# Two first weight loads moved from the SyncE queue to the ScalarE queue, in halves

## The chip, the cores and the metric

The kernel runs on one core of one Trainium2 chip. The core has TensorE (in the profile PE for its matmuls, PEld for its weight loads), VectorE (DVE), ScalarE (ACT), GpSimd (POOL) and SyncE (SP, which here does nothing but issue DMAs). Every engine takes its instructions strictly in order. The metric is the device time of one execution in microseconds (us).

## The reference

Three stages follow one another, all in float32. First windowed attention over 4 batches, 8 heads and 576 positions of 64 values, where a query sees itself and the 63 positions before it:

```
scores = where(mask, scale * q @ k.T, -1e9);  attn = softmax(scores);  x = attn @ v
```

Then, on the 2304 tokens of 512 values, a dense layer with a rational activation:

```
h = x @ w_in                                   # 512 -> 2048
P = a0 + a1*h + a2*h**2 + a3*h**3
Q = 1 + |b0|*|h| + |b1|*h**2
y = (P / (Q + 1e-6)) @ w_out                   # 2048 -> 512
```

Last a mixture of 8 experts, where each token goes to one expert: `out = gate * sigmoid(...) * (relu(y @ w1[e]) @ w2[e])`.

## The kernel before

Tokens are cut into 9 blocks of 256. Attention works in units: a block and a pair of heads, four units to a block, 36 in all. `at_T` transposes q and k of a unit on TensorE (tile `tq`) and copies them out (`kT`, `qbd`, both kept in the tile `KK`), `at_QK` forms the scores (`sc`), masks them on VectorE (`ms`, `mn`, line 343), takes their exponential on ScalarE (line 349) and scales them by the reciprocal of their sum (`sg`, lines 352 and 353, and a product on GpSimd, line 173), `at_PT` transposes them (`pp`), and `at_PV` multiplies by v (`xp`) and stores the block's x as a high and a low part (`x0` for the first block, `xh` and `xl` later).

The dense layer uses split weights: each product is made of three matmuls of high and low parts (`mm3`). So every piece of `w_in` and `w_out` is first loaded raw (tile `stg`, 1 MB, 128 partitions by 2048 words, function `load_w`) and then converted in two halves (`convert`): three VectorE steps on 128x512 words (lines 288, 290, 292; tiles `cp`, then `ct`), a rounding copy for the high part (line 167 or 169) and a difference for the low part (line 173), into `wi` or `wo`. The first half of a raw piece of `w_in` is its tile's first two slices, the second half the last two. There are 16 such pieces; `cseq` gives their order, the first four being pieces of `w_in`.

A step s of the dense layer is one block and one piece: `rt_mm1` (tile `h`), an activation on ScalarE, VectorE and GpSimd (`rt_head`, `rt_inv`, `rt_tail`, `rt_gsplit`, tiles `e`, `t`, `qm`, `r`, `g`), and four steps later `rt_mm2` (tile `y`).

The body at the end of the function emits all this in a written order, with priorities (`later`); a scheduler then lays the instructions of each engine out by a timeline of its own costs, so what stands in a queue is not the written order. Which engine does an operation is fixed while the code is emitted (`pick`). All loads of the first stage stand in SyncE's queue; eight completion semaphores serve the plain DMAs in turn, and a DMA waits until the one before it on its semaphore has landed.

Line 961 loads the first raw weight piece with `c_load(1)`; the second is loaded from `c_conv`, which calls `c_load(m + 1)` and `c_load(m + CA)`. Line 964 is ScalarE's first small operation, the absolute value of the two numbers b.

Of the kernel before, what the change touches and what calls it, by code (L numbers as in the profile page):

```python
# [12 lines left out]
AF = mybir.ActivationFunctionType  # L13
# [23 lines left out]
def kernel(  # L37
# [16 lines left out]
    nc = tc.nc  # L54
# [45 lines left out]
    cs, co, npre, CNT, CN2 = [cols[x] for x in ("cs", "co", "npre", "CNT", "CN2")]  # L100
# [19 lines left out]
    def t8(shape, name, dt=F32R):  # L120
        return w8.tile(shape, dt, tag="w8", name=name)
# [134 lines left out]
    pos = {jf: s for s, jf in reversed(list(enumerate(seq)))}  # L256
    ffirst = [pos[0, fp] for fp in range(NFP)]

    def load_w(n):
        kind, fp = cseq[n]  # L260
        if kind == 0:
            t = t8([128, KD, 512], "stg", U32)
            src = w_in_u[:, fp * 512:(fp + 1) * 512]
        else:
            t = t8([128, 2, 1024], "stg", U32)
            src = w_out_u[fp * 256:(fp + 1) * 256, :]
        nc.sync.dma_start(out=t, in_=src.rearrange("(k p) f -> p k f", p=128))
        for i in range(2):
            r = t[:, 2 * i:2 * i + 2, :] if kind == 0 else t[:, i, :]
            stg[kind, fp, i] = (r[:, :, 0::2], r[:, :, 1::2]) if kind == 0 else (r[:, 0::2], r[:, 1::2])  # L270
# [608 lines left out]
    cpos = [0, 0]  # L879

    def c_load(n):
        while cpos[0] < min(n, len(cseq)):
            load_w(cpos[0])
            cpos[0] += 1
# [25 lines left out]
    def qk_upto(m):  # L910
        while loaded[0] <= min(m, NUNIT // 2 - 1):
            load_qk(loaded[0])
            loaded[0] += 1
# [44 lines left out]
    nc.sync.dma_start(out=cs, in_=cst[:, :C_TRI])  # L958
    v_upto(0)
    qk_upto(1)  # L960
    c_load(1)
    for t in qbd:
        nc.gpsimd.memset(t, 0.0)
    nc.scalar.activation(out=co[:, 4:6], in_=co[:, 4:6], func=AF.Abs)

    def prepare():
        wgs = t2([128, KD, 2 * E], "wgs")
# [194 lines left out]
```

## Time and profile before

| | us |
|---|---|
| median of 3 runs | 808.91 (808.74 to 809.58) |
| the profiled execution | 810.46 |
| its span, first to last instruction | 808.5 |
| TensorE busy | 766.3 |
| VectorE busy | 539.0 |
| ScalarE busy | 506.3 |
| GpSimd busy | 449.9 |

The span is what the profile covers; 2.0 us of the profiled execution lie around it. A share of busy time is a mean over stages with different limits, so the tables by stretch below matter more than these sums. In the timeline, the number in square brackets is how long the engine sat idle before the instruction, and the name behind the arrow is what ended the idle time.

### The profile page before, as it was taken

What the parts mean: (1) busy time and instruction counts of PE and PEld (TensorE: products, weight loads), DVE (VectorE), ACT (ScalarE), POOL (GpSimd) and SP (SyncE); (2) the same over time, 40 slices, a digit from 0 to 9 for tenths busy, and PEclk for the clock granted to TensorE, in tenths of its full rate; (3) what the DMA queues carried; (4) which work ended last, traced back from release to release, by engine and by line L of the source; (5) the groups of instructions that cost most, each with busy time, mean ns of one, the idle gap of its engine ahead of it and who ended that gap; (6) DMA issues with size and microseconds to landing.
All of it is one profiled execution on the core that took longest, in us unless ns stands there. A gap on an engine that the chain in (4) does not pass through costs nothing. (4 is left out here: it accounts for less than half of the span.)

```text
span 808.5 us, 15245 instructions
## 1 busy us (share of the span) xinstructions
PE 766.3 (95%) x5456; PEld 690.8 (85%) x5456; DVE 539.0 (67%) x1289; ACT 506.3 (63%) x1122; POOL 449.9 (56%) x399
## 2 busy tenths in 40 slices
PE   5868999999999999999999999897998999999994
PEld 4758899888899899999999998786997999999993
DVE  5799999876776766666676667465655456654630
ACT  5889786997766686676676665673525555543420
POOL 2596786665555555565654654675523554556430
PEclk9999999999999999999999999998998999999997
DMA  9786351422321211112120000323618777767610
GB/s 227 223 234 180 92 183 79 131 77 57 84 67 27 51 54 37 41 53 53 27 67 14 1 27 1 101 84 97 243 50 328 273 234 213 239 228 257 212 55 14
DMA packets 105602, 95.26 MB, mean 118 GB/s; under 512 B 77424, under 2 KB 77808, under 8 KB 105520
## 3 DMA queue, kind: packets, MB, share of 16 engines
q1 hardware_dynamic: 101840, 84.49, 35.1%
q0 software_dynamic: 3680, 9.73, 3.2%
q8 instruction: 45, 0.74, 0.4%
q14 instruction: 37, 0.30, 0.1%
HBM read 83.02 MB, written 11.44 MB: 117 GB/s over the span
## 5 line engine op out<-in xcount | busy, mean ns | idle before, releaser
L178 PE MATMUL y<-wo,g 128*128 128x512 f32 x864 | 220.1, 402 | 4.3 <-POOL g L173 3.3
L178 PE MATMUL h<-xh,wi 128*128 128x256 f32 x1024 | 195.8, 284 | 0.0
L178 PEld LDWEIGHTS y<-wo,g 128*128 128x128 f32 x864 | 158.4, 191 | 35.8 <-POOL g L173 3.5
L178 PEld LDWEIGHTS h<-xh,wi 128*128 128x128 f32 x1024 | 164.4, 192 | 2.7 <-DVE xl L388 0.2
L178 PE MATMUL h<-xl,wi 128*128 128x256 f32 x512 | 145.9, 285 | 0.0
L173 POOL TENSOR_TENSOR wx<-wr,wx 128x1024 fp32r<-128x1024 f32 x31 | 83.6, 2707 | 59.8 <-ACT wx L167 51.2
L173 POOL TENSOR_TENSOR g<-t,g 128x512 fp32r<-128x512 f32 x72 | 93.0, 1294 | 40.1 <-ACT g L167 34.8
L178 PE MATMUL hp<-xdh,wx 128*128 128x256 f32 x576 | 109.9, 290 | 3.8 <-ACT xdh L786 3.7
L173 POOL TENSOR_TENSOR qm<-qm,e 128x512 f32<-128x512 f32 x72 | 93.4, 1297 | 35.7 <-ACT qm L420 32.2
L178 PE MATMUL yp<-wx,hT 128*128 128x512 f32 x432 | 101.9, 392 | 0.0
L178 PEld LDWEIGHTS h<-xl,wi 128*128 128x128 f32 x512 | 98.3, 192 | 2.5
L178 PEld LDWEIGHTS hp<-xdh,wx 128*128 128x128 f32 x576 | 93.9, 198 | 5.3 <-ACT xdh L786 4.2
L415 ACT ACTIVATE e<-h 128x512 f32<-128x512 f32 x72 | 43.0, 597 | 87.3 <-PE h L178 87.1
L178 PEld LDWEIGHTS yp<-wx,hT 128*128 128x128 f32 x432 | 80.0, 188 | 16.4 <-DVE hT L794 0.3
L173 DVE TENSOR_TENSOR wx<-wr,wx 128x1024 fp32r<-128x1024 f32 x45 | 69.1, 1545 | 26.0 <-ACT wx L167 25.7
L167 ACT CAST wx<-wr 128x1024 fp32r<-128x1024 f32 x68 | 69.2, 1046 | 27.1 <-DMA wr<-in_moe_w_dram 21.8
L178 PE MATMUL hp<-xdl,wx 128*128 128x256 f32 x288 | 83.1, 290 | 0.7 <-DVE xdl L787 0.7
L440 DVE SCALAR_TENSOR_TENSOR t<-t,KK,r 128x512 f32<-128x512 f32 x72 | 53.6, 744 | 41.0 <-ACT r L434 40.6
L422 POOL TENSOR_SCALAR qm<-e,KK 128x512 f32<-128x512 f32 x45 | 34.6, 768 | 49.4 <-ACT e L415 49.2
L426 DVE TENSOR_TENSOR t<-t,h 128x512 f32<-128x512 f32 x72 | 49.1, 681 | 17.1 <-ACT t L416 17.0
L173 POOL TENSOR_TENSOR ms<-ms,sg 128x512 f32<-128x512 f32 (+4 forms) x60 | 39.2, 669 | 37.0 <-DVE sg L353 19.7
L433 ACT ACTIVATE r<-qm,KK 128x512 f32<-128x512 f32 x72 | 49.5, 688 | 15.3 <-POOL qm L173 14.7
(169 smaller groups left out, 1399.3 us busy)
## 6 DMA issues: line engine op xcount, KB each, us to landing
wr<-in_moe_w_dram SPq DMA_DIRECT2D x80, 512.0 KB, 4.8
stg<-in_moe_w_in_dram SPq DMA_DIRECT2D x8, 1024.0 KB, 6.7
stg<-in_moe_w_out_dram SPq DMA_DIRECT2D x8, 1024.0 KB, 7.4
v<-in_v_dram SPq DMA_DIRECT2D x58, 128.0 KB, 2.8
q<-in_q_dram SPq DMA_DIRECT2D x32, 128.0 KB, 2.8
k<-in_k_dram SPq DMA_DIRECT2D x32, 128.0 KB, 2.9
y_dram<-ysb SPq DMA_DIRECT2D x12, 256.0 KB, 2.1
yp_dram<-yq SPq DMA_DIRECT2D x6, 256.0 KB, 2.6
```

What stands on the lines that cost most here:

```text
L167: nc.scalar.copy(out=o, in_=i)
L173: (nc.vector if e == "D" else nc.gpsimd).tensor_tensor(out=o, in0=a, in1=b, op=op)
L178: pe[0] = nc.tensor.matmul(o, lhsT, rhs, start=start, stop=stop).ins
L415: nc.scalar.activation(out=e, in_=h, func=AF.Abs)
L422: (nc.vector if ef == "D" else nc.gpsimd).tensor_scalar(out=qm, in0=e, scalar1=co[:, 5:6], scalar2=co[:, 4:5], op0=ALU.mult, op1=ALU.add)
L426: nc.vector.tensor_tensor(out=t1, in0=t1, in1=h, op=ALU.mult)
L433: nc.scalar.activation(out=r0, in_=qm_t[s], func=AF.Ln, bias=qc_col)
L440: nc.vector.scalar_tensor_tensor(out=t1, in0=t1, scalar=co[:, 0:1], in1=r0, op0=ALU.add, op1=ALU.mult)
```

## The change

The first two raw weight pieces are no longer loaded by SyncE, one DMA of 1 MB each, but by ScalarE, two DMAs of 512 KB each. They stand right behind ScalarE's first small operation, and nothing else of ScalarE may come between (`issue_after`). The first half of a piece is what the first `convert` step reads, the second half what the second reads. The other 14 pieces are loaded by SyncE as before.

```diff
-    def load_w(n):
+    def load_w(n, eng=None):
...
-        nc.sync.dma_start(out=t, in_=src.rearrange("(k p) f -> p k f", p=128))
+        src = src.rearrange("(k p) f -> p k f", p=128)
+        if eng is None:
+            nc.sync.dma_start(out=t, in_=src)
+        else:
+            h = t.shape[1] // 2
+            for i in range(2):
+                eng.dma_start(out=t[:, i * h:(i + 1) * h], in_=src[:, i * h:(i + 1) * h])
...
-    c_load(1)
     for t in qbd:
         nc.gpsimd.memset(t, 0.0)
-    nc.scalar.activation(out=co[:, 4:6], in_=co[:, 4:6], func=AF.Abs)
+
+    with tc.issue_after(nc.scalar.activation(out=co[:, 4:6], in_=co[:, 4:6], func=AF.Abs).ins):
+        for n in range(2):
+            load_w(n, nc.scalar)
+    cpos[0] = 2
```

The scheduler lays the whole first part out anew. Lines below `load_w` move down by 6 in the changed program (9 at the end of the function), so line 288 becomes 294, and 343 becomes 349. VectorE's queue from its first copy of v, before:

```order
L169 COPY v<-v 64x256
L157 COPY KK<-tq 128x256
L159 TENSOR_SCALAR KK<-tq 64x4x64
L169 COPY v<-v 64x2x256
L169 COPY v<-v 64x256
L159 TENSOR_SCALAR KK<-tq 64x4x64
L343 ISA ms,mn<-sc,KK 128x64
```

and now:

```order
L169 COPY v<-v 64x256
L157 COPY KK<-tq 128x256
L159 TENSOR_SCALAR KK<-tq 64x4x64
L294 TENSOR_SCALAR cp<-stg 128x512
L159 TENSOR_SCALAR KK<-tq 64x4x64
L169 COPY v<-v 64x2x256
L169 COPY v<-v 64x256
L296 SCALAR_TENSOR_TENSOR cp<-stg,cp 128x512
L294 TENSOR_SCALAR cp<-stg 128x512
L349 ISA ms,mn<-sc,KK 128x64
```

The conversion of the first piece now begins ahead of the first unit's masks and ahead of one of the two copies of q (`qbd`) that line 159 makes. ScalarE's queue at its start, with what each row waits for, before:

```order
L964 ACTIVATE KK<-KK 128x2 [waits DMASW0_49]
L161 COPY KK<-tq 128x256 [waits PE_49]
L167 COPY v<-v 64x256 [waits DMAHW5_49]
L163 ACTIVATE KK<-tq 64x4x64 [waits DVE_49,Pool_49]
L163 ACTIVATE KK<-tq 64x4x64 [waits DVE_49]
```

and now:

```order
L970 ACTIVATE KK<-KK 128x2 [waits DMASW0_49]
L273 DMA stg<-in_moe_w_in_dram 128x2x512
L273 DMA stg<-in_moe_w_in_dram 128x2x512 [waits DMAHW0_49]
L273 DMA stg<-in_moe_w_in_dram 128x2x512 [waits DMAHW2_49]
L273 DMA stg<-in_moe_w_in_dram 128x2x512 [waits DMAHW4_49]
L167 COPY v<-v 64x256 [waits DMAHW5_49]
L161 COPY KK<-tq 128x256 [waits PE_49]
L163 ACTIVATE KK<-tq 64x4x64 [waits DVE_49,Pool_49]
```

Four DMAs stand ahead of ScalarE's copies, and the copy of v stands ahead of the copy of k. SyncE's queue where the second, third and fourth piece were loaded, before:

```order
L226 DMA k<-in_k_dram 128x4x64 [waits DMAHW5_49]
L267 DMA stg<-in_moe_w_in_dram 128x4x512 [waits DMAHW6_49]
L267 DMA stg<-in_moe_w_in_dram 128x4x512 [waits DMAHW7_49]
L226 DMA q<-in_q_dram 128x4x64 [waits DMAHW4_49,DMAHW5_49,DMAHW0_49,PE_49]
L226 DMA k<-in_k_dram 128x4x64 [waits DMAHW2_49,DMAHW3_49,DMAHW1_49,PE_49]
L226 DMA k<-in_k_dram 128x4x64
L226 DMA q<-in_q_dram 128x4x64
L267 DMA stg<-in_moe_w_in_dram 128x4x512
L267 DMA stg<-in_moe_w_out_dram 128x2x1024
```

and now:

```order
L226 DMA q<-in_q_dram 128x4x64 [waits DMAHW0_49]
L269 DMA stg<-in_moe_w_in_dram 128x4x512 [waits DMAHW1_49]
L226 DMA q<-in_q_dram 128x4x64 [waits DMAHW2_49]
L226 DMA k<-in_k_dram 128x4x64 [waits DMAHW3_49]
L226 DMA k<-in_k_dram 128x4x64 [waits DMAHW4_49]
L226 DMA q<-in_q_dram 128x4x64 [waits DMAHW5_49]
L269 DMA stg<-in_moe_w_in_dram 128x4x512 [waits DMAHW6_49]
L269 DMA stg<-in_moe_w_out_dram 128x2x1024 [waits DMAHW7_49]
```

Here the third piece stands behind q and k of the third pair of units instead of two pieces standing there, and the loads of q and k of the fourth pair no longer wait for TensorE.

## Rows read from the trace of the kernel before

**Rows 1.** The page: span, and busy time of each engine (share, instructions).

```profile
span 808.5 us, 15245 instructions
PE 766.3 (95%) x5456; PEld 690.8 (85%) x5456; DVE 539.0 (67%) x1289; ACT 506.3 (63%) x1122; POOL 449.9 (56%) x399
```

**Rows 2.** Busy time by stretch: stretch, its length, engines (instructions), granted clock, DMA share, GB/s.

```profile
core 0: us, PE busy (x) PEld busy (x) DVE busy (x) ACT busy (x) POOL busy (x), PEclk, DMA share, GB/s
...
10.00:20.00 10.00, 8.18 (x42) 7.40 (x42) 7.97 (x38) 7.64 (x26) 2.68 (x6) 0.90 1.25 266
20.00:30.00 10.00, 8.30 (x90) 6.78 (x88) 5.55 (x21) 8.25 (x32) 5.13 (x8) 0.93 0.97 298
30.00:40.00 10.00, 9.23 (x82) 8.39 (x83) 10.00 (x34) 8.39 (x29) 4.59 (x4) 1.00 0.49 159
40.00:60.00 20.00, 14.12 (x130) 12.16 (x128) 19.24 (x58) 17.11 (x51) 18.13 (x21) 1.00 0.87 228
60.00:80.00 20.00, 17.32 (x159) 15.84 (x160) 18.14 (x58) 19.78 (x65) 13.43 (x19) 0.91 0.73 190
...
100.00:200.00 100.00, 99.03 (x702) 89.34 (x701) 85.40 (x180) 84.40 (x182) 65.30 (x59) 1.00 0.33 105
7.63:32.48 24.85, 19.25 (x153) 16.31 (x153) 18.09 (x69) 18.43 (x65) 8.83 (x17) 0.93 1.09 293
...
4.79:7.28 2.49, 1.80 (x8) 1.43 (x8) 0.17 (x1) 0.01 (x2) 0.18 (x1) 1.00 1.11 234
```

**Rows 3.** Timeline of VectorE, 7 to 33 us: start, duration, instruction, [idle before <-releaser].

```profile
7.63 0.28 DVE L169 COPY v<-v 64x256 f32<-64x256 f32 x1 [2.03 <-DMA v<-in_v_dram]
...
8.18 0.41 DVE L159 TENSOR_SCALAR KK<-tq 64x256 f32<-64x256 f32 x1
...
11.30 0.23 DVE L343 CUSTOM_DVE_ANT_0 ms<-sc,KK 128x64 f32<-128x64 f32 x1 [1.51 <-PE sc L178]
...
12.25 1.29 DVE L288 TENSOR_SCALAR cp<-stg 128x512 uint32<-128x512 uint32 x2
...
18.00 0.22 DVE L343 CUSTOM_DVE_ANT_0 ms<-sc,KK 128x64 f32<-128x64 f32 x1 [0.52 <-PE sc L178]
...
22.43 0.17 DVE L352 TENSOR_SCALAR sg<-sg 128x4 f32<-128x4 f32 x1 [2.37 <-ACT ms L349]
...
27.41 0.17 DVE L352 TENSOR_SCALAR sg<-sg 128x4 f32<-128x4 f32 x1 [2.04 <-ACT ms L349]
...
27.49 0.69 DVE L288 TENSOR_SCALAR cp<-stg 128x512 uint32<-128x512 uint32 x1
...
31.80 0.68 DVE L292 SCALAR_TENSOR_TENSOR ct<-stg,cp 128x512 uint32<-128x512 uint32 x1
```

**Rows 4.** SyncE's queue, 0 to 26 us: DMA issues.

```profile
3.35 1.06 SPq L237 DMA_DIRECT2D v<-in_v_dram  x2
...
5.76 1.20 SPq L267 DMA_DIRECT2D stg<-in_moe_w_in_dram  x1
...
15.98 1.13 SPq L267 DMA_DIRECT2D stg<-in_moe_w_in_dram  x2
```

**Rows 5.** Tile `stg`, 0 to 60 us: SyncE's issue (ns, min/median/max); then, 0 to 10 us, the first piece's landing.

```profile
L267 SPq DMA_DIRECT2D stg<-in_moe_w_in_dram x4: 507/543/1198, 5.8 to 25.0; - x4
...
DMA to landing us min/median/max: 6.4/6.4/6.4
```

**Rows 6.** Tile `q`, 0 to 10 us: from issue to landing.

```profile
DMA to landing us min/median/max: 2.4/3.8/5.8
```

**Rows 7.** Timeline of ScalarE: its first operation, its first copy, and one wait at 44 us.

```profile
4.59 0.20 ACT L964 ACTIVATE KK<-KK 128x2 f32<-128x2 f32 x1 [2.56 <-DMA KK<-in_moe_b_dram]
...
7.28 0.37 ACT L161 COPY KK<-tq 128x256 f32<-128x256 f32 x1 [2.48 <-PE tq L308]
...
44.54 0.37 ACT L387 CAST xh<-xp 128x256 fp32r<-128x256 f32 x1 [1.35 <-PE xp L178]
```

**Rows 8.** Timeline of TensorE: its last long wait of the first part.

```profile
61.45 1.24 PE L178 MATMUL xp<-ms,v 128*64 128x64 f32 x32 [3.77 <-DVE t L442]
```

## Prediction

> **What bounds the kernel now.** I read the page first: TensorE is busy 766.3 of 808.5 us [rows 1]. The table by stretch says where the other 42 us lie. From 100 us on TensorE is full (99.03 of 100), while VectorE and ScalarE are busy some 85% [rows 2]: nothing that this change touches can matter there, except by letting TensorE arrive earlier. Before that TensorE waits: it is idle 1.82, 1.70, 0.77, 5.88 and 2.68 us in the stretches from 10 to 80 us [rows 2]. For whom is seen in the same rows: VectorE has no idle time at all from 30 to 40 us (10.00 of 10) and 0.76 us from 40 to 60; ScalarE is full from 60 to 80 (19.78 of 20). TensorE's longest wait there, 3.77 us at 61.45, ends with a VectorE step of the activation [rows 8]. So up to about 60 us VectorE sets the pace.
>
> Now the stretch before, VectorE's own timeline [rows 3]. From its first copy at 7.63 to the end of the second piece's last conversion step at 31.80 + 0.68 = 32.48 us it is busy 18.09 of 24.85 us [rows 2]: 6.76 us idle. Four waits make 6.44 of it: 1.51, 0.52, 2.37 and 2.04, two for scores, two for exponentials. While it waits there is conversion work that it could do, but the second piece is issued only at 15.98 [rows 4], and its first step runs at 27.49, directly behind the last of the four waits. The first piece was issued at 5.76 and took 6.4 us to land [rows 4, 5], so at 12.16, and its first step runs at 12.25: it too came as early as the load let it.
>
> **What the change does to the order.** What each engine does is unchanged: both programs have the same instructions on VectorE, ScalarE and GpSimd, apart from ScalarE's four DMAs. Only their order differs, and only at the front: the last 4,881 of 6,075 instructions in TensorE's queue, and the last 918 of 1,386 in VectorE's, stand alike. TensorE has 702 matmuls in the 100 us from 100 on [rows 2], so the common part begins somewhere near 160 to 175 us. As TensorE is full there, the end of the kernel moves by what TensorE's arrival moves. So the sum is what VectorE gains before 60 us.
>
> **The sum.** The new order has both loads' steps spread through the front of VectorE's queue: by the fourth `ct` it holds eight steps of the first two pieces ahead of the second reciprocal, against four before. The work to that point is the same but for one step, one x difference and four small operations that come later now; these cancel if both programs are compared at equal work. So VectorE would be 6.76 us earlier if it never stopped, and each stop in the new order is taken off.
>
> First stop: the step on the first half, now the fourth instruction from 7.63, behind `qbd`'s copy, which ends at 8.18 + 0.41 = 8.59 [rows 3]. ScalarE's first operation ends at 4.59 + 0.20 [rows 7], so the half is issued at about 4.85. The shortest landing of a small load there is 2.4 us [rows 6], the whole piece took 6.4 [rows 5]; half of the 4.0 between them added to 2.4 makes 4.4, so it lands at 9.2: 0.6 us lost. Bounds: nothing, if it lands by 8.59; 2.7, if it takes the whole piece's 6.4.
>
> Second stop: the masks of the third unit. Its scores stand behind the first unit's product with v in TensorE's queue now, so VectorE reaches them early. Bounds: nothing and 2.37, the longest wait of the four; I take the middle, 1.2.
>
> Third: later in the front the differences of x wait for ScalarE's casts of the third and fourth unit. In the trace such a cast waited 1.35 us for TensorE at 44.54 [rows 7]; the bounds are zero and what is left of the lead. I take 1.35, the one row of the kind.
>
> Fourth: the transfers. The second piece's 1.05 MB go ahead of loads of q, k and v that stood before them; at the 266 GB/s of that stretch [rows 2] that is 3.9 us, the upper bound. The lower is nothing, or less: the third pair's q and k now stand ahead of the third piece, and the fourth pair's no longer wait for TensorE. I take 0.8, near the lower end, because 10 to 20 us is the stretch in which none of the engines is full.
>
> ScalarE's issuing costs 4 x 0.543 = 2.2 us [rows 5] (no DMA of ScalarE's is in the trace; the bounds are 4 x 0.507 = 2.0 and 4 x 1.198 = 4.8). It lies between 4.79 and 7.28, in which ScalarE is busy 0.01 of 2.49 us [rows 2]: nothing. At 4.8 the first copy of k would begin 2.3 us late.
>
> 6.76 - 0.6 - 1.2 - 1.35 - 0.8 = 2.8 us. TensorE's idle time from 40 to 80 us, 8.56 us, has room for it. So has ScalarE's: it was idle 1.75 + 1.61 + 2.89 = 6.25 us from 20 to 60 us. The profiled execution took 810.46, 1.96 around its span; 808.5 - 2.8 = 805.7 for the span and 807.7 for such an execution. The median of the runs lies 1.55 below the profiled one: 808.9 - 2.8 = 806.1 us.
>
> All of it by bounds: no stop but the second's middle gives 6.76 - 1.2 = 5.6, so 803.3; every stop at its upper end (2.7, 2.37, 1.35, 3.9, and 2.3 for ScalarE) gives 12.6, a loss of 5.9.
>
> The stretch from 10 to 20 us has a DMA share over 1 [rows 2], so the engines that move the data have no room there. On that, "DMA: Bandwidth & Descriptors" of the Trainium skill (section Issuing engines are not separate DMA queues) speaks against this change: DMAs of several issuing engines interleave on the same 16 DMA engines, and a second issuer saves only the issue time. By that rule the gain from issuing is a few issues of 0.54 us; the rest of a gain would have to come from the place in the order. The trace of before has one issuer of such loads and can't show it.
>
> **Rivals.** *The transfers give it back (25%).* Two pieces are in flight at 7 us instead of one, and everything behind them lands up to 3.9 us later. For it: the full DMA share. Against it: from 15.98 on two pieces in a row were in flight before as well, and VectorE's waits were for scores and exponentials, not for loads. The fourth term at its upper end instead of 0.8: 6.76 - 0.6 - 1.2 - 1.35 - 3.9 = -0.3 lost, so 809 us, no change.
>
> *VectorE stands in order behind late halves: slower (15%).* Steps on the four halves now stand ahead of the masks of the first two units, which nothing held before. If the loads of SyncE and ScalarE took equal turns, 133 GB/s would be left for the halves: 0.52 MB then takes 3.9 us, and with 2.4 us ahead of them they land at 11.2, 15.1, 19.1 and 23. The second half's first step stands ahead of the first unit's masks, which ran at 11.30 [rows 3]: these would be 3.8 us late, and the second piece's steps would hold VectorE again. The fourth half's first step has some 8 us of VectorE's work ahead of it, so by 23 it would have been idle 23 - 7.63 - 8 = 7.4 us for the halves alone, and with the second and third terms 10 against 6.76: some 3 us slower, 812. It decides from the second half landing at about 14.4: 2.8 us past 11.6, where VectorE comes to it (9.2 and 2.4 us of steps). Against it: rows of weights are 2 KB in one piece and those of q, k and v 256 bytes, and 293 GB/s moved from 7.63 to 32.48 [rows 2]. The page named above (section Queues, rings and completion order) says that each DMA engine takes turns between the queues with work, packet by packet; by turns of equal size that is this rival, by turns of whole rows the weights come first.
>
> *ScalarE takes VectorE's place (part of the first case).* It is full from 60 us, so a lead of VectorE beyond what ScalarE can follow is lost. Its room of 6.25 us says that 2.8 passes; if its casts fall behind by the 2.2 us of issuing after all, 0.6 is left, 808.3.
>
> **How the numbers follow.** The forecast has 60%: 806.1, from 803.3 to 807.5. The first rival with its part 25%, 807 to 810; the slower one 15%, 809.5 to 813. About 0.2%, 1.6 us, is what a measurement of this kernel can tell from no change. Faster than 807.3: nearly all of the forecast's case and a little of the first rival's, 0.61. Within 1.6 us: 0.26. Slower than 810.5: most of the last case, 0.13. The range leaves out the best end and most of the slower case: 803.6 to 810.0.
>
> **What would show it.** Right: VectorE's steps on the first two pieces done by about 27 us instead of 32.5; its idle time from 7.63 to there nearer 2 than 6.76; TensorE's idle time from 40 to 80 us near 5.8 instead of 8.56; and the same distance from about 170 us to the end. First term: the first conversion step at 9.2, not past 10. Fourth: transposes of the third pair's q and k without a wait for a DMA. Wrong: the first unit's masks past 14 us with VectorE waiting for `stg`; or VectorE early and ScalarE full from 40 us on with TensorE as idle as before; or, against the whole argument, a different time in the part of the queues that stands alike.

## The result and the profile after

The changed kernel is 1.35% slower: 820.20 us median of 4 runs (818.56 to 820.83) against 809.25 of 4 runs of the kernel before (808.74 to 810.56), ratio 1.0135, 95% interval 1.0117 to 1.0152. Forecast were 806.1 us and a range of 803.6 to 810.0. The profiled execution took 820.49 us, with a span of 818.7.

Busy time by stretch of the changed kernel, columns as in [rows 2]:

```profile
7.63:32.48 24.85, 17.54 (x120) 14.81 (x121) 18.66 (x76) 17.25 (x61) 8.22 (x16) 1.00 1.04 287
10.00:20.00 10.00, 6.10 (x26) 5.41 (x27) 8.87 (x34) 5.43 (x22) 2.10 (x6) 1.00 1.09 286
40.00:60.00 20.00, 15.67 (x156) 14.12 (x158) 17.57 (x56) 17.84 (x53) 15.97 (x17) 0.93 0.83 212
60.00:80.00 20.00, 13.89 (x140) 12.31 (x136) 20.00 (x61) 17.09 (x53) 14.69 (x21) 0.93 0.58 154
80.00:100.00 20.00, 18.38 (x99) 15.15 (x98) 10.36 (x27) 9.19 (x28) 8.97 (x12) 0.81 0.40 98
100.00:200.00 100.00, 99.38 (x725) 90.28 (x724) 88.25 (x176) 85.16 (x181) 67.15 (x59) 1.00 0.36 112
```

The same stretch from 80 us in the kernel before, which was not shown above:

```profile
80.00:100.00 20.00, 20.00 (x150) 17.48 (x149) 19.38 (x41) 14.13 (x35) 15.80 (x19) 1.00 0.36 94
```

TensorE is idle 4.33 + 6.11 = 10.44 us from 40 to 80 us, where 8.56 were to shrink to 5.8, and 1.62 more behind 80, where it had no idle time. From 100 us on it is as full as before. The loss is therefore complete before the common part of the queues begins, and one small ScalarE operation of the router shows it well: the first `og`, which both programs reach inside the part in which TensorE is full. Here in the kernel before, then in the changed one (start, duration):

```profile
213.56 0.20 ACT L572 ACTIVATE og<-og 128x2 f32<-128x2 f32 x1
```

```profile
222.81 0.20 ACT L578 ACTIVATE og<-og 128x2 f32<-128x2 f32 x1
```

9.25 us later; the span is 10.2 longer. (The way from the first `og` to the end is not the same length in every execution, though the queues stand alike there: it took 594.9 us before and 595.9 in the changed kernel, and 591.7 to 595.9 over the thirteen executions in the table below whose row there is the same, all but n1 and n5. So the span of one execution decides nothing below some 4 us.) What lies in front of it is TensorE's timeline. The kernel before, 73 to 90 us (rows of `h` left out):

```profile
73.10 0.98 PE L178 MATMUL xp<-ms,v 128*64 128x64 f32 x16 [0.78 <-ACT ms L161]
74.52 0.63 PE L363 MATMUL pp<-KK,ms 128*128 128x128 f32 x4 [0.44 <-DVE mn L343]
74.90 3.02 PE L178 MATMUL y<-wo,g 128*128 128x512 f32 x12
...
80.63 1.09 PE L178 MATMUL y<-wo,g 128*128 128x512 f32 x4
81.66 0.98 PE L178 MATMUL xp<-ms,v 128*64 128x64 f32 x16
...
83.92 4.35 PE L178 MATMUL y<-wo,g 128*128 128x512 f32 x18
```

The changed kernel, 76 to 95 us:

```profile
76.08 0.98 PE L178 MATMUL xp<-ms,v 128*64 128x64 f32 x16 [1.05 <-ACT ms L161]
79.29 0.69 PE L314 MATMUL tq<-KK,k 128*128 128x128 f32 x2 [2.23 <-DVE mn L349]
...
80.31 1.09 PE L369 MATMUL pp<-KK,ms 128*128 128x128 f32 x4
83.03 1.52 PE L178 MATMUL xp<-ms,v 128*64 128x64 f32 x16 [1.62 <-ACT ms L161]
84.47 9.98 PE L178 MATMUL y<-wo,g 128*128 128x512 f32 x36
```

Before, the y matmuls are filler: runs of 12, 4 and 18 stand between the attention steps, and TensorE does not wait at all from 74.9 to 100. In the new order three more attention steps come first, TensorE waits 1.05, 2.23 and 1.62 us among them, and the first 36 y's follow in one run. And the clock falls, in the changed kernel and then in the one before over the same stretch:

```profile
77.50:87.80 10.30, 6.89 (x32) 5.15 (x33) 8.68 (x22) 7.75 (x24) 6.66 (x8) 0.50 0.46 130
```

```profile
77.50:87.80 10.30, 10.30 (x75) 8.93 (x74) 9.82 (x26) 9.30 (x27) 8.97 (x12) 1.00 0.38 103
```

A granted clock of 0.50 is the 1.2 GHz level; it came after the wait of 1.05 us and during that of 2.23. 16 matmuls of `xp` take 1.52 us there instead of 0.98.

### The profile page after: what moved, and what is told of

The parts are those of the page before. It is cut to its first block, busy times and chain, and to the rows that moved or that the text cites. A ratio compares the mean times of both kernels' runs of the same rounds, so it can differ in the third digit from the quotient of the medians.

```text
span 818.7 us, 15224 instructions
## 1 busy us (share of the span) xinstructions
PE 769.3 (94%) x5456; PEld 692.1 (85%) x5456; DVE 542.0 (66%) x1289; ACT 505.9 (62%) x1122; POOL 449.6 (55%) x399
## 5 line engine op out<-in xcount | busy, mean ns | idle before, releaser
L178 PEld LDWEIGHTS y<-wo,g 128*128 128x128 f32 x864 | 160.6, 193 | 35.8 <-POOL g L173 3.6
L173 DVE TENSOR_TENSOR wx<-wr,wx 128x1024 fp32r<-128x1024 f32 x45 | 73.1, 1634 | 25.6 <-ACT wx L167 25.3
L167 ACT CAST wx<-wr 128x1024 fp32r<-128x1024 f32 x68 | 69.3, 1047 | 27.4 <-DMA wr<-in_moe_w_dram 22.2
L355 ACT ACTIVATE ms<-ms,mn 128x128 f32<-128x128 f32 (+1 forms) x144 | 55.7, 391 | 5.7 <-DVE mn L349 2.8
```

The lines of the kernel that those rows point to most:

```text
L167: nc.scalar.copy(out=o, in_=i)
L173: (nc.vector if e == "D" else nc.gpsimd).tensor_tensor(out=o, in0=a, in1=b, op=op)
L178: pe[0] = nc.tensor.matmul(o, lhsT, rhs, start=start, stop=stop).ins
L355: nc.scalar.activation(out=ms[:, i, :nk[i]], in_=ms[:, i, :nk[i]], func=AF.Exp, scale=-1.0, bias=mn[:, i:i + 1], accum_out=sg[:, i:i + 1])
```

## The experiments

In most of them the order of the instructions on every engine (the "row") is held by hand, so that it can be kept while something else is changed. Each instruction is made to follow its neighbour in a list at the end of the file; the rest is the changed kernel:

```diff
+            line = [have[i] for i in order]
+            for a, b in zip(line, line[1:]):
+                tc.add_manual_dep(b, a.name, info, reason="hold")
```

| kernel | row | first loads | ratio to before (95%) | first `og`, us |
|---|---|---|---|---|
| before | its own | SyncE | 1 | 213.6 |
| changed | its own | ScalarE, halves | 1.0135 (1.0117 to 1.0152) | 222.8 |
| e1 | before | ScalarE, halves | 1.0001 (0.9978 to 1.0024) | 215.0 |
| e4 | changed | SyncE, whole | 1.0116 (1.0065 to 1.0167) | 224.9 |
| e2 | changed, v copies later | ScalarE, halves | 1.0102 (1.0053 to 1.0151) | 223.0 |
| h46 | changed to 46 us, then before | ScalarE, halves | 1.0015 (0.9991 to 1.0040) | 214.6 |
| h54 | to 54 us | ScalarE, halves | 0.9979 (0.9938 to 1.0019) | 213.6 |
| h66 | to 66 us | ScalarE, halves | 1.0048 (1.0022 to 1.0075) | 218.2 |
| h74 | to 74 us | ScalarE, halves | 1.0027 (0.9999 to 1.0054) | 218.3 |
| e5 | changed, 12 y's earlier | ScalarE, halves | 1.0065 (1.0043 to 1.0087) | 219.2 |
| e6 | e5, `sc` earlier | ScalarE, halves | 1.0075 (1.0047 to 1.0103) | 216.8 |
| e7 | e6, masks earlier | ScalarE, halves | 1.0038 (1.0012 to 1.0065) | 215.7 |
| n1 | planner's own | ScalarE, whole | 1.0121 (1.0092 to 1.0150) | 220.9 |
| n5 | planner's own | SyncE, whole | 1.0115 (1.0079 to 1.0151) | 222.2 |
| e8 | before, unpacking earlier | ScalarE, halves | 1.0034 (1.0014 to 1.0054) | 214.6 |

The last column is of one profiled execution each; the ratio decides. The times given below for "before" are its median in the same measurement.

**e1: the row of before, the loads of the change.** The list holds the order of before for all five engines; ScalarE's four DMAs stay.

> Nothing is left out. Every engine's instructions are held in the row in which the kernel before has them; only the first two weight loads differ, which ScalarE issues in halves behind its Abs, as in the changed kernel. Theory ORDER (what costs the 11 us is the new row of instructions that the planner makes after the edit, above all between 50 and 95 us): 806 to 811 us, near the kernel before, though the first copy of v still ends late. Theory CROWDING (what costs is that the halves on the second queue delay the first rows of v, k and q, and all engines start 2.5 us late): 815 to 820 us, near the changed kernel, with the first copy of v at about 10.1 us. Theory CLOCK (the stretches at the 1.2 GHz level between 77 and 88 us cost): goes with ORDER here, and those stretches are gone.

811.51 us against 810.84: no difference, with an interval of 1.9 us either way (the band for ORDER ended at 811). The edit by itself costs nothing and gains nothing that this interval can tell. The first copy of v was early, not late; but the loads do crowd another one, the k of the third unit, for which the transposes now wait (start, duration, [wait]):

```profile
14.52 0.44 PE L316 MATMUL tq<-KK,k 128*128 128x128 f32 x2 [1.82 <-DMA k<-in_k_dram]
```

**e4: the row of the change, the loads of before.** In the list of the changed kernel's order the two loads stand, whole, on SyncE behind its first eight DMAs:

```diff
-            load_w(n, nc.scalar)
+            load_w(n)
```

> Nothing is left out. Every engine's instructions are held in the row of the changed kernel, but the first two weight loads are whole again and issued by SyncE behind its first eight loads, so ScalarE issues none and v is not crowded. Theory CROWDING: 808 to 812 us, near the kernel before, with the first copy of v at about 7.6 us. Theory ORDER: 816 to 821 us, near the changed kernel, though the first copy of v is early, and TensorE idles and falls to its lower clock between 75 and 90 us again.

821.68 us, just above the band for ORDER: as slow as the changed kernel with nothing on ScalarE's queue. v is there at 7.43 us, and TensorE stands before the y's as it did:

```profile
85.10 1.52 PE L178 MATMUL xp<-ms,v 128*64 128x64 f32 x16 [3.31 <-ACT ms L161]
86.55 9.98 PE L178 MATMUL y<-wo,g 128*128 128x512 f32 x36
```

With e1 this settles the main question: the row costs some 10 us, the place of the loads nothing that these runs can tell.

**e2: v out of the way.** Only the first copies of v on VectorE and ScalarE are moved behind those of k and q.

```diff
 VectorE
-COPY v<-v 64x256
 COPY KK<-tq 128x256
 TENSOR_SCALAR KK<-tq 64x4x64
 ...
+COPY v<-v 64x256
```

> Nothing is left out. The changed kernel in its own row of instructions, but the first copies of v on VectorE and ScalarE stand behind the first copies of k and q, so that those do not wait for a late v. Theory CROWDING: VectorE's and ScalarE's first work begins 2 us earlier and most of the loss is won back, 809 to 814 us. Theory ORDER: the row behind 50 us is unchanged, 817 to 821 us, even where the first masks end earlier.

820.25 us. In the profiled execution of the changed kernel v had landed late, at 10.10 us instead of 7.63 [rows 3], and I had taken that for a cause. VectorE's first copy there:

```profile
10.10 0.28 DVE L169 COPY v<-v 64x256 f32<-64x256 f32 x1 [4.70 <-DMA v<-in_v_dram]
```

In the thirteen other profiled executions that copy v first it began between 7.08 and 7.71 us, and seven of them have the same loads in the same order. It was one execution's accident, and moving v wins nothing that shows.

**h54, h66, h74, h46: where in the row.** Each engine keeps the changed kernel's order up to what it had begun at 54 (66, 74, 46) us and takes what is left in the order of before.

```diff
-line = order of the changed kernel
+line = (its first n of each engine) + [the rest in the order of before]
```

> Nothing is left out. The changed kernel with ScalarE's loads in halves; each engine keeps the changed kernel's row up to what it has begun at 54 us, and from there takes what is left in the row of the kernel before. Theory ORDER, with the costly part behind 54 us: 805 to 811 us. Theory CROWDING, or ORDER with the costly part in front of 54 us: 816 to 821 us.

808.27 us against 810.84: the whole loss is gone, so it lies behind 54 us. In this kernel the first 12 y's start at 75.33 us, 0.4 behind before:

```profile
74.01 0.98 PE L178 MATMUL xp<-ms,v 128*64 128x64 f32 x16 [0.97 <-ACT ms L161]
75.33 2.99 PE L178 MATMUL y<-wo,g 128*128 128x512 f32 x12
```

Whether it beats the kernel before stays open: its interval takes in 1.

> Nothing is left out. ScalarE's loads in halves; each engine keeps the changed kernel's row up to what it has begun at 66 us there, and takes the rest in the row of the kernel before. Theory LATE (the loss arises behind 66 us, where TensorE waits in front of the 36 y's): 806 to 812 us. Theory MID (it arises between 54 and 66 us, where TensorE waits 2.84, 1.10 and 1.32 us): 814 to 820 us.

> Nothing is left out. As the kernel cut at 66 us, but cut at 74 us: only what begins behind 74 us stands in the row of before, the 12 y's in front of the waits at 77 us among it. Theory LATE: 807 to 813 us, and at least 5 us less than the changed kernel. Theory MID: 815 to 821 us, the loss being in the row by then.

> Nothing is left out. As the kernel cut at 54 us, but cut at 46 us: from there every engine has the row of the kernel before. Theory ORDER: 803 to 810 us, at most 0.2% above the kernel before. If the halves on ScalarE's queue do win time in front of 46 us, as was predicted, and the row of before keeps it, it is 0.2 to 0.6% below the kernel before; if the gain is lost behind 46 us in any row, it is within 0.2%.

813.87, 812.44 and 811.02 us against 809.70. The first lies between its two bands, 1.9 us above LATE and 0.1 below MID, so by itself it decides for neither. The second is in LATE's, and it stays some 1% below the changed kernel's ratio. So the row from 54 to 74 us carries some 0.3 to 0.5%, 2 to 4 us (the intervals allow 0 to 0.75%), and what begins behind 74 us most of the loss, some 7 to 9 of the 11. h46 is 1.0 us above its band in us and, at 0.15% over before, inside the one in per cent. It gains nothing over before: no gain of the loads that these runs can tell was hidden in front of 46 us.

**e5, e6, e7: the filler.** e5 moves 12 of the 36 y's on TensorE, in the row of the change; e6 also puts four `sc` in front of the other 24; e7 also puts four masks of VectorE in front of three unpacking steps.

```diff
 TensorE (e5)
 MATMUL xp<-ms,v 64x64 x8
+MATMUL y<-wo,g 128x512 x12
 MATMUL tq<-KK,k 128x128 x2
 ...
-MATMUL y<-wo,g 128x512 x36
+MATMUL y<-wo,g 128x512 x24
```

> Nothing is left out. The changed kernel, every instruction in its row, but for one move on TensorE: of the 36 matmuls into y that begin at 84.47 us there, the first 12 stand in front of the transposes that wait from 77.06 to 79.29 us. Theory FILLER (the loss arises where TensorE waits with y's ready behind the waiting instruction): the wait of 2.23 us goes, the clock does not fall there or for less long (at most some 3 us more), so 813 to 817 us. Theory WHOLE ROW (the loss is spread over the row of all engines behind 54 us, VectorE's above all, and the y's place is only its sign): 818 to 821 us, with the wait found again elsewhere before 90 us.

> Nothing is left out. As the kernel with the 12 y's moved, and the four sc matmuls that stand behind the h's at 97.16 us in the changed kernel are moved in front of the remaining 24 y's, so that VectorE, which idles 7.55 us for them, has its next masks about 10 us earlier. If VectorE's idle stretch there costs TensorE later (theory CHAIN): 2 to 5 us less than with the y's alone, 809 to 814 us. If TensorE is the bound from there on and VectorE's idle time is free: within 1 us of the kernel with the y's alone.

> Nothing is left out. As the kernel with the 12 y's and the four sc matmuls moved on TensorE, and on VectorE the four masks that stand between three conversions from 76.6 to 79.2 us stand in front of those three (1.9 us earlier). If VectorE's conversions among the masks carry the rest of the loss: TensorE's wait of 1.63 us for ms goes and the time falls by 1.5 to 4 us, 809 to 813 us. If not: 813 to 816 us, as without it.

e5: 815.88 us against 809.77. The ratio, 1.0065, is half of the changed kernel's 1.0135; against e2, the same row held with only v moved, 1.0102 shrank by a little over a third, and there the intervals overlap. So a third to a half of the loss goes with one move on one engine. The wait of 2.23 us is gone, though the granted clock is still 0.63 from 77.10 to 81.70, the lower level over most of the first 12 (4.61 us; 3.02 for as many before):

```profile
76.19 0.98 PE L178 MATMUL xp<-ms,v 128*64 128x64 f32 x16 [1.32 <-DVE t L435]
77.10 4.61 PE L178 MATMUL y<-wo,g 128*128 128x512 f32 x12
81.54 0.38 PE L316 MATMUL tq<-KK,k 128*128 128x128 f32 x2
...
84.20 0.98 PE L178 MATMUL xp<-ms,v 128*64 128x64 f32 x16 [1.63 <-ACT ms L161]
85.11 5.74 PE L178 MATMUL y<-wo,g 128*128 128x512 f32 x24
```

e6 (814.88 us against 809.77) is the same within the intervals, but it is no test of whether VectorE's idle time beside the y's costs anything. From 76 to 100 us VectorE was idle 24 - 16.51 = 7.49 us in e5 and 24 - 16.52 = 7.48 in e6: its longest wait there was 3.09 us for `sc` in e5 (up to 93.98 us), and it is 4.12 for ScalarE in e6 (up to 93.51).

e7 lies at 813.23 us against 809.70. The wait of 1.63 that it aimed at is still there, so its mechanism is refuted, and whether it is really 0.3% faster than e6 the intervals leave open:

```profile
80.71 0.98 PE L178 MATMUL xp<-ms,v 128*64 128x64 f32 x16 [1.63 <-ACT ms L161]
```

**n1, n5: the planner left free.** In n1 ScalarE issues each load in one piece; n5 issues at the same place in the program, but on SyncE.

```diff
 n1
-            h = t.shape[1] // 2
-            for i in range(2):
+            h = t.shape[1]
+            for i in range(1):
 n5
-            load_w(n, nc.scalar)
+            load_w(n)
```

> Nothing is left out. The changed kernel, but ScalarE issues each of the two loads whole and not in halves; the planner is left free and makes yet another row (the first y's in runs of 22, 18 and 8, with attention between them). Theory ORDER: the time goes by that row and not by who issues, anything from 804 to 816 us, and its excess over the kernel before equals TensorE's idle time up to 100 us over that before (20.06 us) plus what the half clock takes. Theory CROWDING (the second queue itself costs): 816 to 821 us.

> Nothing is left out. SyncE issues both loads whole, at the place in the program where the changed kernel has them, so no second queue; the planner is left free and makes its own row (first y's in two runs of 24, behind four attention steps). Theory ORDER: slower than before although no load is on ScalarE's queue, 811 to 821 us, with TensorE waiting in front of the first y's. Theory CROWDING: 807 to 811 us.

818.48 and 819.69 us against 809.77. Each small edit gets another row, with the first y's in runs of 22, 18 and 8 or of 24 and 24, and both rows are about 1% worse than that of before, with or without a second queue. n1 came out 2.5 us above the band that I gave for ORDER and inside CROWDING's; what speaks against CROWDING is e1, with ScalarE's loads and no loss, and n5, as slow with no load on ScalarE. The sum that I offered for n1 (idle time of TensorE to 100 us, and what the lower clock takes) can't be tested with these numbers: to 100 us n1 was busy 77.09 us against 79.94 before and reached `og` 7.3 us later, but h54 was busy 81.90 and reached `og` when before did, so busy time there does not count work (the part on the gain, below, shows why). Much of n5's loss is seen in its stretch from 60 to 80 us, in waits (6.77 us, where before had 2.68) and the lower clock:

```profile
60.00:80.00 20.00, 13.23 (x129) 11.75 (x128) 18.21 (x50) 15.47 (x48) 13.23 (x19) 0.74 0.33 90
```

**e8: VectorE's lead by force.** Open was why the forecast 2.8 us do not come in e1 either. e8 is e1 with the second load's four unpacking steps moved into VectorE's two long waits.

```diff
 VectorE
 SCALAR_TENSOR_TENSOR ct<-stg,cp 128x512
+TENSOR_SCALAR cp<-stg 128x512 x2
 TENSOR_SCALAR sg<-sg 128x4
 ...
+SCALAR_TENSOR_TENSOR cp<-stg,cp 128x512 x2
 TENSOR_SCALAR sg<-sg 128x4
-TENSOR_SCALAR cp<-stg 128x512 (x2), SCALAR_TENSOR_TENSOR cp<-stg,cp 128x512 x2
```

> Nothing is left out. The kernel in the row of before with ScalarE's loads in halves, and one move on VectorE: the four operations that unpack the second load (0.60 us each, 2.4 us, behind VectorE's second wait for ScalarE's ms at 27.41 us in the kernel before) stand in its two waits, two in front of the wait of 2.37 us that ends at 22.43 us and two in front of the one of 2.04 us that ends at 27.41 us. So VectorE is really 2.4 us ahead from 32 us on. Theory of the prediction (the end follows VectorE's lead): 2 to 3 us less than the kernel before, ratio 0.996 to 0.998. Theory ATTENTION (from 32 us on the end hangs on the attention steps and on x, which no earlier weight moves): within 0.2% of the kernel before, with the first activation of h less than 1 us earlier than in the same row without the move (47.1 us).

812.04 us against 809.25: not faster but 0.34% slower (0.14 to 0.54), so ATTENTION's band of 0.2% is missed as well, and whether it is slower than e1 the intervals leave open. The first activation of h runs at 47.1 us, as in e1. VectorE's waits, start, duration, [wait]:

```profile
24.52 0.17 DVE L360 TENSOR_SCALAR sg<-sg 128x4 f32<-128x4 f32 x1 [0.96 <-ACT ms L357]
...
29.54 0.17 DVE L360 TENSOR_SCALAR sg<-sg 128x4 f32<-128x4 f32 x1 [0.88 <-ACT ms L357]
...
31.73 0.42 DVE L396 TENSOR_TENSOR x<-xp,x 128x256 fp32r<-128x256 f32 x1 [1.38 <-ACT x L395]
```

The two waits (2.17 and 2.05 us in e1) shrink by as much as was put into them, 1.2 us each, and a third appears at once: VectorE runs up against the casts of x, which come out of attention. Of the lead of 2.4 us some 0.3 is left at the next piece, whose first unpacking step runs at 34.70 us instead of 35.03. A lead of VectorE does not reach the end. Besides, the third unit's transposes wait for k (1.12 us; 1.82 in e1). The landing of the k loads (shortest, median, longest) in the first 12 us, in the kernel before and in e8:

```profile
DMA to landing us min/median/max: 2.9/3.6/5.8
```

```profile
DMA to landing us min/median/max: 3.2/5.6/8.2
```

## Why the prediction was wrong

**The step that failed** is the one from the order to the sum: "As TensorE is full there, the end of the kernel moves by what TensorE's arrival moves. So the sum is what VectorE gains before 60 us." The first sentence held: `og` came 9.25 us later, and the end 10.2. The second did not follow. Behind 60 us, up to the point from which both queues stand alike, the row was new too, and I gave that part no term. e4 shows that the loss comes with the row, h54 that all of it lies behind 54 us, h74 that most of it begins behind 74, and e5 that a third to a half of it is the place of 12 matmuls. The order was at hand: 36 y's in one run behind three more attention steps. In the trace of before the two steps in front of the first y's had waited for ScalarE and VectorE (0.78 and 0.44 us), and those with y's in front of them had not.

**The gain.** VectorE idled 24.85 - 18.66 = 6.19 us from 7.63 to 32.48, not the 2 that I expected, against 6.76 before. But 2.47 of the 6.19 are the late v of that one execution. In h46 and h54, with the same front row and an early v, it idled 24.85 - 19.98 = 4.87 and 24.85 - 17.54 = 7.31 us:

```profile
7.63:32.48 24.85, 17.90 (x128) 15.26 (x128) 19.98 (x79) 18.44 (x68) 9.59 (x17) 0.93 1.10 297
```

```profile
7.63:32.48 24.85, 20.16 (x116) 17.79 (x117) 17.54 (x73) 16.48 (x59) 7.62 (x14) 1.00 1.09 296
```

The two differ in the pace of TensorE, first h46, then h54:

```profile
21.19 1.13 PE L178 MATMUL sc<-KK 128*128 128x64 f32 x8 [0.37 <-DVE KK L159]
```

```profile
21.36 2.08 PE L178 MATMUL sc<-KK 128*128 128x64 f32 x8
```

The granted clock reads 1.00 from 20 to 28 us in both, so it does not show this; why the pace rose later in h54 is open. h54 is none the slower at the end for it.

The weights were unpacked earlier: the last `ct` of the second piece ended at 28.8 us in h54 and 27.4 in h46, instead of 32.48. It did not help. First cast of x: 22.37 us before, 22.41 in h46, 22.47 in h54, 24.18 in e1. TensorE's first h stood at 24.54 before, behind a wait of 1.51 us for VectorE's rounding copy of the first piece, and comes no earlier than 24.99 in any other run. In h46 TensorE itself reaches it only at 24.83 (then waits 0.41). Measured at that point the sum's 2.8 is zero or less.

**Term one, the halves' landing (9.2 us).** A little late: in the seven executions with the new front row and an early v the first step on a half began at 9.46 to 10.12 us, behind a wait of 0.63 to 1.69 where the term had 0.6. The rival's 11.2 by equal turns of the two queues is not seen in them, and in e8 all four halves had landed 8.3 us after issue or sooner while the loads of k took 2 us longer than before (the medians, 5.6 and 3.6). On that, "DMA: Bandwidth & Descriptors" of the Trainium skill (section Queues, rings and completion order) lets each DMA engine take turns between the queues with work, packet by packet. The traces agree with turns in which the weights, with rows of 2 KB, move more than k with rows of 256 bytes; the size of a turn no run shows.

**Term two, the third unit's masks (1.2 us).** Mis-sized. VectorE now has three unpacking steps in front of the first masks, and TensorE has a transpose of probabilities (`pp`) between the third unit's transposes of q and k. In h54, VectorE's and then TensorE's timeline:

```profile
9.81 0.69 DVE L296 TENSOR_SCALAR cp<-stg 128x512 uint32<-128x512 uint32 x1 [1.35 <-DMA stg<-in_moe_w_in_dram]
...
12.83 0.21 DVE L351 CUSTOM_DVE_ANT_0 ms<-sc,KK 128x64 f32<-128x64 f32 x1
...
19.58 0.42 DVE L157 COPY KK<-tq 128x256 f32<-128x256 f32 x1 [1.77 <-PE tq L316]
...
23.48 0.23 DVE L351 CUSTOM_DVE_ANT_0 ms<-sc,KK 128x64 f32<-128x64 f32 x1 [1.42 <-PE sc L178]
```

```profile
15.21 0.66 PE L316 MATMUL tq<-KK,k 128*128 128x128 f32 x2 [2.12 <-DMA k<-in_k_dram]
16.99 0.42 PE L371 MATMUL pp<-KK,ms 128*64 128x128 f32 x1 [1.12 <-POOL ms L173]
17.20 0.42 PE L316 MATMUL tq<-KK,k 128*128 128x128 f32 x1
```

The first masks run at 12.83 us instead of 11.30, and those of the third unit at 23.48 instead of 18.00 [rows 3] (22.36 in h46, where TensorE was faster): the third unit is 4.4 to 5.5 us late. VectorE stops for it more than once, 1.77 us for its transposes and 1.42 for its scores (1.77 and 0.36 in h46), so some 2.1 to 3.2 us where the term had 1.2.

**Term four, the transfers (0.8 us).** Too small in the row of before: behind the halves the third unit's k is waited for 1.82 us in e1 and 1.12 in e8, where TensorE had not waited for it, and in e1 x comes 1.8 and `og` 1.5 us later. In the new row the wait of 2.12 in h54 costs nothing that shows: the `pp` behind it runs at 16.99 us, and at 16.93 in h46, which does not wait for k.

**Term three** (the casts of x, 1.35 us) has no wait of its own in h46 or h54; in e8 the one wait of the kind was 1.38. Nor was 1.35 the one row of the kind: two casts of the first block's x waited 1.19 and 0.37 us for TensorE in the trace of before. **ScalarE's issuing at no cost** held: its four issues took 2.57 us from 4.42 in the changed kernel, and with them e1 is as fast as before.

**The rivals.** The slower one had the sign, not the mechanism: from its first step on a half on, VectorE has no wait for `stg` up to 40 us in the changed kernel. The transfers giving the gain back comes nearest to e1, whose x and `og` are 1.8 and 1.5 us late and whose time is that of before. Neither priced the order behind 60 us. By "DMA: Bandwidth & Descriptors" of the Trainium skill (section Issuing engines are not separate DMA queues) a second issuer saves only issue time. e1's 1.0001 agrees.

What stays open: the rest of the loss, half of it or more, which no single move among those tried gives back; how much of it is the lower clock, since no run kept the waits and the clock apart; and whether h54's 0.2% is a gain.

## What to carry to other kernels

Where a planner writes the order, an edit of two lines changes the order of everything up to the point where both programs stand alike, and that is what has to be priced: go through the new order of the engine that bounds the end, look for instructions that waited in the trace, and see whether the work that used to stand between them still does. To learn what an edit is worth in itself, hold the old order and change only the edit (here 1.0001 against 1.0135). And filling another engine's idle time is a gain only if it makes early what the bound engine waits for last. Here TensorE's long waits from 50 to 80 us were for attention steps and a step of the activation (in e8 1.72 us for the masks' `mn` and 2.01 for `t`), not for weights.

## What the runs showed of the hardware

The same loads in the same order brought the first v at 10.10 us in one execution and at 7.11 to 7.64 in seven others: a wait for a DMA in one trace is worth a second execution before it is called a cause. And TensorE's lower clock makes a wait dearer than it looks: in the stretch of 10.3 us at the 1.2 GHz level, 16 matmuls of `xp` took 1.52 instead of 0.98 us, and in e5, at a mean granted clock of 0.63, the 12 y's took 4.61 instead of 3.02, 1.6 us lost in work that did not wait. A granted clock of 1.00 does not say that the pace is full, either: eight `sc` took 2.08 us in h54 and 1.13 in h46, both at 1.00, so near the start of the program a busy time is not yet a measure of work.
